# Two running-sum products for each tile's branch, of the tokens' high part and of the rest plus k1 times the first sum, in place of three products of gated operands

## The chip, the cores and the metric

The kernel runs on one core of a Trainium2 chip. A core has TensorE (matrix products into PSUM), VectorE, ScalarE and GpSimd (element-wise work), SyncE (here it only issues DMAs), and DMA engines between the chip's memory (HBM) and the on-chip memory (SBUF). Each engine runs its own list of instructions in order and waits on semaphores for the others. The metric is the device time of one execution in microseconds (us), lower is better.

## The reference

Input are 2048 tokens of 448 channels. With six modulation rows from a conditioning vector `c`, the reference is

```
h = layernorm(x) * (1 + ca) + sa
x = x + ga * (causal_conv(h, K) + h * Dskip)
h = layernorm(x) * (1 + cb) + sb
x = x + gb * ((silu(h @ w_gate) * (h @ w_up)) @ w_down)
```

`K[d, l]` is the real part of a sum over 256 states of `C * dt * B * exp(dt * A * l)`. For inputs whose `dt * A` is very small (the kernel computes a flag for it), `K` is a straight line in `l`: `k0 + k1 * l` for each channel. Then, with t the token of the output and s the token of the input,

```
conv(h)[t] = sum over s <= t of (k0 + k1 * (t - s)) * h[s]
```

which needs only running sums over the tokens. This is the path that runs here. A second path (an FFT by matrix products) lies behind the flag and isn't executed.

## The kernel before

**Tiling.** The 2048 tokens are 16 tiles of 128 tokens, tokens on the partitions and the 448 channels along the row. Tiles go in six blocks (`TILES`): 0-1, 2-3, 4-6, 7-9, 10-12, 13-15. A prologue computes `k0` and `k1` multiplied by the gate `ga` (rows `gm0`, `gm1`, spread over all partitions), the gated skip `gd`, and tiles 0 and 1 entirely up to the transposed operand of the feed-forward part.

**The feed-forward loop.** `run_blocks` calls `ffn` for each block. It has 14 steps f, one for each 128 hidden columns. `gate_up(f)` is 22 matmuls (f32r operands, split into a high and a low part for accuracy) as wide as the block has tokens, 256 or 384; then ScalarE's silu (L773), VectorE's product (L788), ScalarE's cast to the high part `phi` (L795) and VectorE's subtraction for the low part `plo` (L796). `down(f - 1)` is then issued: three 448-wide matmuls for each tile of the block (L808). In the first block the weights arrive during the steps, so that each step also splits weights: ScalarE L115, L122, L123 and VectorE L117 (`wdl`) and L125 (`gu`).

**The branch of the next block** is threaded through these steps. `TIMES` has, for each tile of the next block, a list of half steps h for its stages: an even h places a stage behind `gate_up(h / 2)` and ahead of the `down` that follows it, an odd h behind that `down`. Within one half step the order is tile by tile, then stage by stage. Every engine gets its instructions in exactly this order. The first row of `TIMES` is used while block 0 runs (tiles 2 and 3), the second while block 1 runs (tiles 4 to 6), the third for the later blocks. The last entry of each tile is not a stage but the statistics of its second layernorm.

**The stages before.** `s0` makes the normalized token tile h (VectorE L200, L202, two scalar_tensor_tensor). `s1` makes `v0 = h * gm0` and `v1 = h * gm1` (L957), where row s of `gm0` holds k0 - s * k1 (made once by `gate_0`, L732). `rows` adds to row 0 of both the carried rows (L962, L963). `s2` splits v0 into `vh` (ScalarE L970) and `vl` (VectorE L971). `s3` is h * gd (L976). `s4` multiplies by the triangle of ones `tri`, which is a running sum over the tile's tokens: `vh` and `vl` into the PSUM tile `CV` (L982, L984), `v1` into one of the four rotating PSUM banks (L983); and adds h * gd to x (L985). `s5` copies the last rows, adds them up (L1003, L1004) and sends them by a DMA to partition 0 as the carry for the next tile (L1005; SyncE's queue for tiles 2 and 3, ScalarE's for the others), then adds `o` and `s * token` to x (L1006, L1007).

Which engine multiplies differs by block. While blocks 0 and 1 run, `s1` and `s3` are on VectorE (`v(s1)`, `v(s3)`); later they are on GpSimd. While block 0 runs, tiles 2 and 3 use `s4f`: v0 isn't split but multiplied as full f32 (L995), and v1 as f32r (L994).

**Other names.** `CV` is a single PSUM bank that the branch, `gate_row` and one of the four transposes share. `split_w(j)` and `split_d(j)` split weights, and `pools.load` issues their DMAs on SyncE's queue. `left_over` (name `l1` in `PLAN`) sums `v1` of tiles 0 and 1 for the first carry; `first_rows` and `gate_0` prepare the carry and the gate rows in block 0; `PLAN` is the order of the prologue, written out by hand.

Of the kernel before, what the change touches and what calls it, by code (L numbers as in the profile page):

```python
# [8 lines left out]
F32 = mybir.dt.float32  # L9
F32R = mybir.dt.float32r  # L10
# [33 lines left out]
m1 cpc k1 gd h11 hd0 ck v01 sq0 o10 v10 w0 cbw o12 v11 o01 o02 hd1 w01 o13 o14 fs xh1 gc0 sa d00 gc1 st0 r0 sp x1 st1 r1 l1 spc n10 gq fl n11 D0 qtb sbt sbc  # L44
# [7 lines left out]
def f32(ap):  # L52
    return ap.bitcast(F32)
# [3 lines left out]
def tile_kernel(ctx, tc, x, a_re, a_im, b_re, b_im, c_re, c_im, log_dt,  # L57
# [71 lines left out]
    tok = const.tile([128, 1], F32)  # L129
# [12 lines left out]
    ntok = const.tile([128, 1], F32)  # L142
# [144 lines left out]
    with tc.tile_pool(name="pre", bufs=1) as pre:  # L287
# [20 lines left out]
        po.iota(tok, pattern=[[1, 1]], base=0, channel_multiplier=1, allow_small_or_imprecise_dtypes=True)  # L308
        po.iota(ntok, pattern=[[1, 1]], base=0, channel_multiplier=-1, allow_small_or_imprecise_dtypes=True)
# [25 lines left out]
        for z in range(2):  # L335
# [20 lines left out]
        h01, v0, v1, hd, h2 = ([pre.tile([128, w], t, name=f"{n}_{q}") for q in range(2)] for n, t, w in  # L356
                               (("h", F32, D), ("v0", F32, D), ("v1", F32R, D), ("hd", F32, D), ("h2", F32, 512)))
# [114 lines left out]
        def flag_of():  # L472
# [43 lines left out]
            "fr1": copy(run1[end], CV[end, 0:D]), "fx": copy(xs[0], DN[0][:, 0:D]),  # L516
# [204 lines left out]
    def first_rows():  # L721

        ve.tensor_tensor(run0[end], run1[end], DN[1][end, 0:D], op=OP.add)
# [6 lines left out]
    def gate_0():  # L730

        ve.scalar_tensor_tensor(gm0, gm1, ntok, gm0, op0=OP.mult, op1=OP.add)  # L732

    def run_blocks(pools, stages, first=None):
# [150 lines left out]
        for b, ts in enumerate(TILES):  # L885
            todo = {}
            if b + 1 < len(TILES):
# [53 lines left out]
    def small_path(pools):  # L941
# [10 lines left out]
        def s1(i, on_v=False):  # L952
            h = vs[i]
            v0 = v0_of(i)
            v1 = work.tile([128, D], F32R, name="v1", bufs=2)
            for v, g in ((v0, gm0), (v1, gm1)):
                (ve if on_v else po).tensor_tensor(v, h, g, op=OP.mult)  # L957
            vs[i] = h, v0, v1

        def rows(i):  # L960
            h, v0, v1 = vs[i]
            ve.tensor_tensor(v0[0:1], v0[0:1], run0[0:1], op=OP.add)  # L962
            ve.tensor_tensor(v1[0:1], f32(v1[0:1]), run1[0:1], op=OP.add)  # L963

        def s2(i):
            rows(i)
            h, v0, v1 = vs[i]
            vh = work.tile([128, D], F32R, name="vh")
            vl = work.tile([128, D], F32R, name="vl")
            sc.copy(vh, v0)  # L970
            ve.tensor_tensor(vl, v0, f32(vh), op=OP.subtract)  # L971
            vs[i] = h, vh, vl, v1

        def s3(i, on_v=False):
            h = vs[i][0]
            (ve if on_v else po).tensor_tensor(h, h, gd, op=OP.mult)  # L976

        def s4(i):
            h, vh, vl, v1 = vs[i]
            o = CV[:, 0:D]  # L980
            s = bank()[:, 0:D]
            pe.matmul(o, tri, vh, start=True, stop=False)  # L982
            pe.matmul(s, tri, v1, start=True, stop=True)  # L983
            pe.matmul(o, tri, vl, start=False, stop=True)  # L984
            ve.tensor_tensor(xs[i], h, xs[i], op=OP.add)  # L985
            vs[i] = o, s

        def s4f(i):  # L990
            h, v0, v1 = vs[i]
            o = CV[:, 0:D]
            s = bank()[:, 0:D]
            pe.matmul(s, tri, v1, start=True, stop=True)  # L994
            pe.matmul(o, f32(tri), v0, start=True, stop=True)  # L995
            s3(i, True)
            ve.tensor_tensor(xs[i], h, xs[i], op=OP.add)
            vs[i] = o, s

        def s5(i):  # L1000
            o, s = vs.pop(i)
            if i + 1 < NT:
                sc.copy(run1[end], s[end])  # L1003
                ve.scalar_tensor_tensor(run0[end], run1[end], 128.0, o[end], op0=OP.mult, op1=OP.add)  # L1004
                (sy if i in TILES[1] else sc).dma_start(run[0:1], run[127:128])  # L1005
            ve.tensor_tensor(xs[i], xs[i], o, op=OP.add)  # L1006
            ve.scalar_tensor_tensor(xs[i], s, tok, xs[i], op0=OP.mult, op1=OP.add)  # L1007

        v = lambda g: lambda i: g(i, True)
        return lambda b: ((s0, v(s1), rows, s4f, s5), (s0, v(s1), s2, v(s3), s4, s5),  # L1010
                          (s0, s1, s2, s3, s4, s5))[min(b, 2)]

# [104 lines left out]
```

## Time and profile before

| what | value |
|---|---|
| median of 3 runs (lowest to highest) | 471.73 us (470.73 to 472.09) |
| profiled execution, its own time | 471.05 us |
| its span, first to last instruction | 468.9 us |
| granted TensorE clock, mean | 0.999 |
| end of the prologue, first matmul of the feed-forward part | 31.18 us |
| blocks 0 and 1 (256 tokens each) end at about | 85.5 and 141 us |
| blocks 2, 3, 4 (384 tokens each) end at about | 220.5, 301 and 381.5 us |

The profile's columns: start and duration in us, the engine, the line of the kernel, the operation, output and inputs by the names of the tiles, how many instructions the row merges, and in brackets how long the engine sat idle before it and who released it. Starts of two instructions that follow each other on one engine are often closer than the duration of the first, since instructions overlap in the engine's pipeline; where a stretch of work is added up, the distance of starts is the price.

### The profile page before, as it was taken

How to read it: one execution, taken by the hardware profiler on the slowest of the kernel's cores; microseconds unless marked ns; L12 is line 12 of the kernel's file. 1: busy time of each engine (PE TensorE's matmuls, PEld its weight loads, DVE VectorE, ACT ScalarE, POOL GpSimd, SP SyncE). 2: the span in 40 equal slices, each digit the busy share in tenths (PEclk: the TensorE clock that was granted, in tenths of full speed). 3: DMA queues.
4: the chain of work that ended last, by engine and by line, in shares of the span. 5: the costliest groups of instructions: out<-in, count | busy, mean ns of one | idle time of the engine just before them, and what ended most of it. 6: DMA issues, size and time to landing. Idle time of an engine off the chain costs nothing.

```text
span 468.9 us, 7027 instructions
## 1 busy us (share of the span) xinstructions
PE 459.8 (98%) x2735; PEld 438.2 (93%) x2735; DVE 282.0 (60%) x539; ACT 160.7 (34%) x363; POOL 64.2 (14%) x88
## 2 busy tenths in 40 slices
PE   7899999999999999999999999999999999999995
PEld 5579999999999999999999999999999999999995
DVE  5888999778865547573745756464666553222125
ACT  5888665522243122233212233321223222221111
POOL 2232001000000224100032410004141000000000
PEclk9999999999999999999999999999999999999999
DMA  8966652200003000111300011130000112000001
GB/s 319 404 242 210 219 166 74 67 33 2 2 0 100 0 1 0 46 46 46 117 2 0 2 45 46 45 119 1 1 23 24 46 45 80 22 1 1 1 0 64
DMA packets 18779, 31.24 MB, mean 67 GB/s; under 512 B 2609, under 2 KB 13489, under 8 KB 18737
## 3 DMA queue, kind: packets, MB, share of 16 engines
q1 hardware_dynamic: 18096, 30.53, 18.8%
q8 instruction: 23, 0.38, 0.3%
q10 hardware_dynamic: 640, 0.18, 0.2%
q14 instruction: 20, 0.16, 0.1%
HBM read 24.61 MB, written 6.03 MB: 65 GB/s over the span
## 4 chain that ended last, share of the span: by engine, by line
PE 94%; issue 1%; DVE 1%; DMA 1%; POOL 1%; ACT 1%; DVEq 0%; POOLq 0%; ACTq 0%
PE bank L758 61%; PE dn L808 28%; DMA vec<-in_c_log_dt_dram 1%; PE dn L480 1%; PE bank L983 1%; PE cv L984 1%; PE cv L982 1%; PE bank L227 0%; PE bank L266 0%; DVE x L847 0%; PE bank L403 0%; POOL rsa L186 0%; PE cv L995 0%; PE bank L437 0%; ACT L339 0%
## 5 line engine op out<-in xcount | busy, mean ns | idle before, releaser
L758 PE MATMUL bank<-hhi,gu 128*128 128x384 f32 (+1 forms) x1176 | 208.8, 317 | 0.1
L758 PEld LDWEIGHTS bank<-hhi,gu 128*128 128x128 f32 x1176 | 189.3, 188 | 2.9 <-issue 0.8
L758 PE MATMUL bank<-hlo,gu 128*128 128x384 f32 (+1 forms) x672 | 130.7, 317 | 0.0
L758 PEld LDWEIGHTS bank<-hlo,gu 128*128 128x128 f32 x672 | 109.0, 188 | 0.2
L788 DVE TENSOR_TENSOR bank<-raw,bank 128x384 f32<-128x384 f32 (+1 forms) x69 | 36.9, 534 | 117.5 <-PE bank L758 115.2
L795 ACT CAST phi<-bank 128x384 fp32r<-128x384 f32 (+1 forms) x83 | 36.8, 444 | 138.2 <-DVE bank L788 138.1
L773 ACT ACTIVATE raw<-bank 128x384 f32<-128x384 f32 (+1 forms) x70 | 32.9, 470 | 119.1 <-PE bank L758 103.5
L796 DVE TENSOR_TENSOR plo<-bank,phi 128x384 fp32r<-128x384 f32 (+1 forms) x83 | 42.5, 512 | 37.6 <-ACT phi L795 37.6
L808 PE MATMUL dn<-wdh,phi 128*128 128x448 f32 x218 | 57.6, 365 | 0.0
L808 PE MATMUL dn<-wdh,plo 128*128 128x448 f32 x218 | 57.2, 363 | 0.0
L808 PE MATMUL dn<-wdl,phi 128*128 128x448 f32 x218 | 56.9, 362 | 0.0
L808 PEld LDWEIGHTS dn<-wdh,plo 128*128 128x128 f32 x218 | 40.8, 188 | 3.0 <-DVE plo L796 0.4
L808 PEld LDWEIGHTS dn<-wdl,phi 128*128 128x128 f32 x218 | 40.9, 187 | 2.7
L808 PEld LDWEIGHTS dn<-wdh,phi 128*128 128x128 f32 x218 | 38.7, 188 | 1.6 <-ACT p L773 0.2
L185 POOL TENSOR_SCALAR rsb<-mvb 128x1 f32<-128x1 f32 (+2 forms) x13 | 4.4, 337 | 142.2 <-DVE mvb L157 142.2
L125 DVE TENSOR_TENSOR gu<-raw,gu 128x1024 fp32r<-128x1024 f32 x14 | 17.1, 1220 | 0.9 <-ACT gu L123 0.9
L185 POOL TENSOR_SCALAR rsa<-mva 128x3 f32<-128x3 f32 (+1 forms) x6 | 2.3, 380 | 99.2 <-DVE mva L157 96.9
L957 POOL TENSOR_TENSOR m<-m,gm 128x448 f32<-128x448 f32 x9 | 10.4, 1154 | 20.8 <-DVE m L202 17.1
L971 DVE TENSOR_TENSOR vl<-m,vh 128x448 fp32r<-128x448 f32 x12 | 9.1, 757 | 6.7 <-ACT vh L970 6.1
L122 ACT CAST gu<-raw 128x768 fp32r<-128x768 f32 x14 | 11.7, 832 | 0.0
L976 POOL TENSOR_TENSOR m<-m,gd 128x448 f32<-128x448 f32 x9 | 11.6, 1283 | 0.0
L215 ACT ACTIVATE raw<-raw,rsb 128x64 f32<-128x64 f32 x14 | 4.8, 345 | 18.9 <-DVE raw L212 9.7
(237 smaller groups left out, 413.9 us busy)
## 6 DMA issues: line engine op xcount, KB each, us to landing
raw<-in_B_w_gate_up_dram SPq DMA_DIRECT2D x14, 512.0 KB, 3.6
rawd<-in_B_w_down_dram SPq DMA_DIRECT2D x16, 224.0 KB, 3.8
x<-in_A_u_dram SPq DMA_DIRECT2D x12, 224.0 KB, 2.9
out_dram<-x SPq DMA_DIRECT2D x11, 224.0 KB, 2.0
xd<-raw SPq DMA_DIRECT2D x9, 256.0 KB, 2.1
raw<-xd SPq DMA_DIRECT2D x36, 64.0 KB, 1.9
wm<-in_w_mod_groups_dram SPq DMA_DIRECT2D x5, 448.0 KB, 8.2
wm<-in_w_mod_groups_dram SPq DMA_DIRECT2D x5, 336.0 KB, 8.2
```

The lines of the kernel that those rows point to most:

```text
L122: sc.copy(wgu[j][:, :, 0:3, :], w[:, :, 0:3, :])
L125: ve.tensor_tensor(wgu[j][:, :, 3:7, :], w[:, :, ::-1, :], f32(wgu[j][:, :, 0:4, :][:, :, ::-1, :]), op=OP.subtract)
L185: po.tensor_scalar(rs[:, 0:n], self.mv[:, 0:n, 1], EPS, None, op0=OP.add)
L758: pe.matmul(ps[s][:, 0:n], w[:, s, a], (hlo if lo else hhi)[:, k, first_col(n):first_col(n) + n], start=first and q == 0, stop=end and q = ...
L773: sc.activation(p[:, 0:n], ps[0][:, 0:n], AF.Silu)
L788: ve.tensor_tensor(ps[1][:, 0:n], p[:, 0:n], ps[1][:, 0:n], op=OP.mult)
L795: sc.copy(hi[:, 0:n], ps[1][:, 0:n])
L796: ve.tensor_tensor(lo[:, 0:n], ps[1][:, 0:n], f32(hi[:, 0:n]), op=OP.subtract)
L808: pe.matmul(dn[q][:, 0:D], u[:, cs], v, start=f == 0 and z == 0, stop=f == (NF - 3 if last else NF - 1) and z == 2)
L957: (ve if on_v else po).tensor_tensor(v, h, g, op=OP.mult)
L971: ve.tensor_tensor(vl, v0, f32(vh), op=OP.subtract)
L976: (ve if on_v else po).tensor_tensor(h, h, gd, op=OP.mult)
```

## The change

For each tile the two sums are now chained. With u the running sum of h, the convolution is (k0 - k1) * u[t] + k1 * (running sum of u)[t]. So:

- `s1` (GpSimd, all blocks): `v0 = h * gd`.
- `s2`: the carried row is added to row 0 of h (VectorE), `hh` is the high part of h (ScalarE cast), and h becomes the rest, h - hh (VectorE).
- `s3` (GpSimd): the rest is multiplied by `gm0`, and `v0` is added to x.
- `s4`: one product, `u = tri * hh`, into `CV`.
- `s5`: VectorE makes `t = u * gm1`, `w = t + h` (the gated rest) and adds the second carried row to row 0 of w; the first carry (last row of u) is copied and sent; VectorE makes `t = u * gma` with gma = gm0 - gm1, and GpSimd adds it to x.
- `s6`: the second product, `v = tri * w`, into the same `CV`.
- `s7`: the second carry (last row of v) is copied and sent, and VectorE adds v to x.

All blocks use this list; the variants by block are gone, and so are the index columns `tok` and `ntok`. Two carries are sent for each tile, of one row each, in place of one of two rows. In the prologue, two casts `hh0` and `hh1` on ScalarE feed `left_over`; `gate_0` is three GpSimd instructions in place of one on VectorE; the DMA of the first carry is issued at step 2 in place of step 0. `TIMES` has eight stages for each tile:

```
-    ((1, 3), 5, ((5, 10, 13, 15, 15, 16), (9, 9, 17, 19, 20, 20)), 20, (22, 23)),
-    ((2, 3, 3), 3, ((5, 6, 8, 10, 10, 11, 13), (7, 8, 14, 15, 17, 17, 18), (13, 17, 17, 18, 20, 21, 21)), 23, (23, 23, 23)),
-    ((2, 3, 3), 3, ((5, 6, 8, 9, 10, 11, 12), (7, 8, 13, 14, 15, 16, 17), (11, 12, 18, 18, 20, 21, 21))),
+    ((1, 3), 5, ((5, 6, 10, 11, 12, 12, 14, 15, 16), (9, 10, 14, 15, 16, 16, 18, 20, 20)), 20, (22, 23)),
+    ((2, 3, 3), 3, ((5, 5, 8, 8, 10, 10, 12, 13, 13), (7, 8, 12, 12, 14, 14, 16, 17, 18), (11, 12, 16, 16, 18, 18, 20, 21, 21)),
+     23, (23, 23, 23)),
+    ((2, 3, 3), 3, ((5, 5, 8, 8, 10, 10, 12, 13, 13), (7, 8, 12, 12, 14, 14, 16, 17, 17), (11, 12, 16, 16, 18, 18, 20, 21, 21))),
...
+    gma = const.tile([128, D], F32)
...
-                pe.matmul(CV[:, 0:D], all1, v1[q], start=q == 0, stop=q == 1)
+                pe.matmul(CV[:, 0:D], all1, hh[q], start=q == 0, stop=q == 1)
...
-            "fr1": copy(run1[end], CV[end, 0:D]), "fx": copy(xs[0], DN[0][:, 0:D]),
+            **{f"hh{q}": copy(hh[q], h01[q]) for q in range(2)}, "fr1": copy(run0[end], CV[end, 0:D]), "fx": copy(xs[0], DN[0][:, 0:D]),
...
-        ve.tensor_tensor(run0[end], run1[end], DN[1][end, 0:D], op=OP.add)
+        ve.tensor_copy(run1[end], DN[1][end, 0:D])
...
-        ve.scalar_tensor_tensor(gm0, gm1, ntok, gm0, op0=OP.mult, op1=OP.add)
+        t = v0_of(2)[end]
+        po.tensor_tensor(gma, gm0, gm1, op=OP.subtract)
+        po.tensor_tensor(t, run0[end], gma[end], op=OP.mult)
+        po.tensor_tensor(run1[end], run1[end], t, op=OP.subtract)
...
-                    at(0, 1, lambda: sy.dma_start(run[0:1], run[127:128]))
+                    at(2, 1, lambda: sy.dma_start(run[0:1], run[127:128]))
...
+        def s1(i):
+            po.tensor_tensor(v0_of(i), vs[i], gd, op=OP.mult)
+
+        def s2(i):
             h = vs[i]
+            ve.tensor_tensor(h[0:1], h[0:1], run0[0:1], op=OP.add)
+            hh = work.tile([128, D], F32R, name="hh")
+            sc.copy(hh, h)
+            ve.tensor_tensor(h, h, f32(hh), op=OP.subtract)
+            vs[i] = h, hh
+
+        def s3(i):
             h = vs[i][0]
+            po.tensor_tensor(h, h, gm0, op=OP.mult)
+            po.tensor_tensor(xs[i], xs[i], v0_of(i), op=OP.add)
 
         def s4(i):
+            h, hh = vs[i]
+            u = CV[:, 0:D]
+            pe.matmul(u, tri, hh, start=True, stop=True)
+            vs[i] = h, u
+
+        def carry(i, k, row):
+            if i + 1 < NT:
+                sc.copy(run[end, k, :], row[end])
+                (sy if i in TILES[1] else sc).dma_start(run[0:1, k, :], run[127:128, k, :])
 
         def s5(i):
+            h, u = vs[i]
+            t = work.tile([128, D], F32, name="t")
+            w = work.tile([128, D], F32R, name="w")
+            ve.tensor_tensor(t, u, gm1, op=OP.mult)
+            ve.tensor_tensor(w, t, h, op=OP.add)
+            ve.tensor_tensor(w[0:1], f32(w[0:1]), run1[0:1], op=OP.add)
+            carry(i, 0, u)
+            ve.tensor_tensor(t, u, gma, op=OP.mult)
+            po.tensor_tensor(xs[i], xs[i], t, op=OP.add)
+            vs[i] = w
+
+        def s6(i):
+            v = CV[:, 0:D]
+            pe.matmul(v, tri, vs[i], start=True, stop=True)
+            vs[i] = v
+
+        def s7(i):
+            v = vs.pop(i)
+            carry(i, 1, v)
+            ve.tensor_tensor(xs[i], xs[i], v, op=OP.add)
+
+        return lambda b: (s0, s1, s2, s3, s4, s5, s6, s7)
```

More of the change, by code (lines that the diff above doesn't have):

```diff
@@ L128, in tile_kernel @@
     tri = const.tile([128, 128], F32R)
-    tok = const.tile([128, 1], F32)
     run = const.tile([128, 2, D], F32)
@@ L141, in tile_kernel @@
     mhalf, half = halves[:, 0:1], halves[:, 1:2]
-    ntok = const.tile([128, 1], F32)
     pick = const.tile([128, 1], F32)
@@ L355, in tile_kernel @@
         sca = pre.tile([128, N], F32)
-        h01, v0, v1, hd, h2 = ([pre.tile([128, w], t, name=f"{n}_{q}") for q in range(2)] for n, t, w in
-                               (("h", F32, D), ("v0", F32, D), ("v1", F32R, D), ("hd", F32, D), ("h2", F32, 512)))
+        h01, v0, v1, hd, hh, h2 = ([pre.tile([128, w], t, name=f"{n}_{q}") for q in range(2)] for n, t, w in
+                               (("h", F32, D), ("v0", F32, D), ("v1", F32R, D), ("hd", F32, D), ("hh", F32R, D), ("h2", F32, 512)))
         qt = {n: pre.tile([128, 512], F32, name="qt" + n) for n in "gcs"}
@@ L948, in s0 @@
             vs[i] = h
-        def s1(i, on_v=False):
+        def s1(i):
+            po.tensor_tensor(v0_of(i), vs[i], gd, op=OP.mult)
+        def s2(i):
             h = vs[i]
[L954 to L974, printed above, removed]
+            ve.tensor_tensor(h[0:1], h[0:1], run0[0:1], op=OP.add)
+            hh = work.tile([128, D], F32R, name="hh")
+            sc.copy(hh, h)
+            ve.tensor_tensor(h, h, f32(hh), op=OP.subtract)
@@ L975, in s3 @@
+            vs[i] = h, hh
+        def s3(i):
             h = vs[i][0]
-            (ve if on_v else po).tensor_tensor(h, h, gd, op=OP.mult)
+            po.tensor_tensor(h, h, gm0, op=OP.mult)
+            po.tensor_tensor(xs[i], xs[i], v0_of(i), op=OP.add)
         def s4(i):
[L979 to L998, printed above, removed]
-        def s5(i):
[L1001 to L1007, printed above, removed]
```

7 lines of the change are left out of this document (1 added, 6 removed).

## The prediction

> **What bounds the kernel now.** I read the page's totals first, then its slices.
>
> ```profile
> PE 459.8 (98%) x2735; PEld 438.2 (93%) x2735; DVE 282.0 (60%) x539; ACT 160.7 (34%) x363; POOL 64.2 (14%) x88
> ...
> PE   7899999999999999999999999999999999999995
> ...
> DVE  5888999778865547573745756464666553222125
> ...
> PE bank L758 61%; PE dn L808 28%; DMA vec<-in_c_log_dt_dram 1%; PE dn L480 1%; PE bank L983 1%; PE cv L984 1%; PE cv L982 1%; PE bank L227 0%; PE bank L266 0%; DVE x L847 0%; PE bank L403 0%; POOL rsa L186 0%; PE cv L995 0%; PE bank L437 0%; ACT L339 0%
> ```
>
> TensorE is the bound from 31 us to the end: the chain is its own matmuls, and the branch's products (L982 to L984, L995) lie on it. Whatever leaves TensorE's list shortens the kernel by its full length, and whatever makes TensorE wait lengthens it. VectorE's 60% is a mean: in slices 3 to 7 (35 to 82 us) it is at 7 to 9 tenths. So I asked for the windows of the blocks.
>
> ```profile
> 31.00:85.50 54.50, 54.37 (x398) 51.66 (x398) 50.68 (x92) 39.11 (x91) 5.42 (x10) 1.00 0.47 154
> 85.50:141.00 55.50, 55.49 (x414) 54.06 (x414) 42.78 (x88) 18.25 (x46) 2.23 (x4) 1.00 0.07 22
> 141.00:220.50 79.50, 79.50 (x440) 77.82 (x439) 44.57 (x81) 20.97 (x44) 14.72 (x17) 1.00 0.11 35
> ```
>
> After the length come TensorE, weight loads, VectorE, ScalarE and GpSimd in us. In block 0 VectorE works 50.7 of 54.5 us, in block 1 42.8 of 55.5, in block 2 44.6 of 79.5. TensorE waits in none of them, and GpSimd does 5.4 and 2.2 us in the first two.
>
> **What it removes: 3.5 us of TensorE.** The chain in order of time gives the steps, and TensorE's timeline the products.
>
> ```profile
> 50.01 2.51 PE bank L758 x22
> 52.52 1.20 PE dn L808 x6
> ...
> 59.93 1.20 PE dn L808 x6
> 61.34 0.75 PE cv L995 x2
> 62.09 2.60 PE bank L758 x22
> ...
> 174.15 1.80 PE dn L808 x9
> 175.95 3.81 PE bank L758 x22
> ```
> ```profile
> 127.58 0.37 PE L982 MATMUL cv<-vh,tri 128*128 128x448 f32 x1
> 127.78 0.36 PE L983 MATMUL bank<-v,tri 128*128 128x448 f32 x1
> ...
> 128.18 0.56 PE L808 MATMUL dn<-wdh,phi 128*128 128x448 f32 x2
> ...
> L984 PE MATMUL cv<-vl,tri 128*128 128x448 f32 x12 | 4.4, 364 | 0.0
> ```
>
> Starts are 0.20 us apart (three products in 0.60), so a product of this kind costs 0.20, three of them 0.60; the new pair has the same shape and type and costs 0.40. Tiles 4 to 15 (x12) save 12 x 0.20 = 2.4 us. Tiles 2 and 3 spend from 59.93 + 1.20 = 61.13 to 62.09, 0.96, and would spend 0.40: 2 x 0.56 = 1.1. Together 3.5 us.
>
> **What it adds on VectorE: a chain between two products.** Before, the products of a tile follow each other. Now the second needs `t`, `w` and the row of `w`, which VectorE can only begin behind the `plo` of that step. The prices, start to start:
>
> ```profile
> 50.83 0.68 DVE L200 SCALAR_TENSOR_TENSOR m<-x,mva,ca 128x448 f32<-128x448 f32 x1
> ...
> 52.26 0.63 DVE L957 TENSOR_TENSOR m<-m,gm 128x448 f32<-128x448 f32 x1
> ...
> 53.34 0.62 DVE L117 TENSOR_TENSOR wdl<-rawd,wdh 128x448 fp32r<-128x448 f32 x1
> ...
> 54.20 1.22 DVE L125 TENSOR_TENSOR gu<-raw,gu 128x1024 fp32r<-128x1024 f32 x1
> ...
> 55.67 0.62 DVE L957 TENSOR_TENSOR m<-m,gm 128x448 f32<-128x448 f32 x1
> ...
> 70.63 1.23 DVE L125 TENSOR_TENSOR gu<-raw,gu 128x1024 fp32r<-128x1024 f32 x1 [0.45 <-ACT gu L123]
> ...
> 105.55 0.60 DVE L962 TENSOR_TENSOR m<-m,run 1x448 f32<-1x448 f32 x1
> ...
> 107.33 0.62 DVE L957 TENSOR_TENSOR m<-m,gm 128x448 f32<-128x448 f32 x1
> ...
> 108.40 0.42 DVE L788 TENSOR_TENSOR bank<-raw,bank 128x256 f32<-128x256 f32 x1
> ...
> 109.60 0.62 DVE L976 TENSOR_TENSOR m<-m,gd 128x448 f32<-128x448 f32 x1
> 110.25 0.63 DVE L985 TENSOR_TENSOR rawd<-m,rawd 128x448 f32<-128x448 f32 x1
> ```
>
> `make_h` costs 1.43 (50.83 to 52.26). Block 0's own work of a step costs 2.33 (53.34 to 55.67), block 1's 1.20 (108.40 to 109.60, with the wait for the cast). Row, cast on ScalarE and rest cost about 1.78 (105.55 to 107.33, two rows then, of which the second ran under the cast). A 448-wide instruction costs 0.54, or 0.66 behind one that it depends on (109.60 to 110.25).
>
> *Block 0*, from `make_h` of tile 3 at 50.83 to the end of tile 3's row of `w`: 1.43; step 5's own work 2.33; tile 2's row, cast and rest 1.78; step 6 2.33; `t`, `w`, row, `t` again 0.66 + 0.66 + 0.53 + 0.54 = 2.39; step 7 2.33; tile 3's row, cast and rest 1.78; x + v 0.54; step 8 2.33; `t`, `w` and the row's end 1.92. That is 19.2 us, or 70.0; plus 0.45 twice, since the cast `hh` waits in ScalarE's list ahead of the weight splits that VectorE needs (the 0.45 at 70.63 is such a wait): 70.9. TensorE would want that product (`s6`, behind `gate_up(9)`) at 52.52 + 4 x 3.71 + 3 x 0.20 = 68.0. **2.9 us late**, shared out over the products on the way.
>
> *Block 1*, counted from the end of `gate_up(5)`, a step being 3.71 + 0.20: 0.1, own work 1.20, tile 4's 2.39, `make_h` of tile 6 1.43, step 6's 1.20, tile 5's row to rest 1.78, then x + v of tile 4, which ends at 8.7. Tile 5's first product writes `CV`, which that addition still reads, and is wanted at 7.8: 0.9 late. The same sum goes on without another wait until tile 6's first product, 0.2 late. **1.1 us.**
>
> *Later blocks*: a step is 5.62 + 0.20. Own work with 384 columns is about 1.20 x 384 / 256 = 1.8 us, the chain 1.92: 2 us of room, which hold tile by tile what else a half step carries. Nothing.
>
> **What it moves to GpSimd.** Four GpSimd instructions of 448 elements for each tile, where blocks 0 and 1 had none. What happens when both engines read SBUF:
>
> ```profile
> 185.07 1.16 POOL L957 TENSOR_TENSOR v<-m,g 128x448 fp32r<-128x448 f32 x1
> 185.54 1.16 DVE L971 TENSOR_TENSOR vl<-m,vh 128x448 fp32r<-128x448 f32 x1 [1.48 <-ACT vh L970]
> 186.18 1.55 POOL L976 TENSOR_TENSOR m<-m,gd 128x448 f32<-128x448 f32 x1
> ...
> L971 DVE TENSOR_TENSOR vl<-m,vh x12: 624/626/1162, 106.8 to 362.2; 128x448 fp32r<-128x448 f32 x12
> ...
> 21.95 1.14 POOL L478 TENSOR_TENSOR hd<-h,gd 128x448 f32<-128x448 f32 x1 [3.36 <-ACT gd L481]
> ...
> 22.60 1.15 DVE L478 TENSOR_TENSOR v<-h,dn 128x448 fp32r<-128x448 f32 x2
> ```
>
> The rest took 1.162 in place of 0.626 beside a GpSimd instruction, and the next GpSimd instruction 1.55 in place of 1.16: VectorE loses 0.54 at a meeting. An operand in PSUM avoids it (22.60: two in 1.15, GpSimd's unhurt). Between 52 and 70 us six of the GpSimd instructions run (`s1` of tile 3, `s3` twice for both tiles, x + t of tile 2), and VectorE is never idle for long: 6 x 0.54 = **3.2 us**. In block 1 VectorE's SBUF-only instructions (row, rest, `w`, row, about 2.1 us of a step of 3.9) fill half the time, and there is room in some steps, so I take half of the delay as reaching a product: 12 x 0.5 x 0.54 x 0.5 = **1.6 us**. Bounds: 0, and every meeting at its full 1.15, 6.9 and 3.5 us. I take 0.54, since L971 is the very instruction.
>
> **Small parts.**
>
> ```profile
> 25.20 0.60 ACT L115 CAST wdh<-rawd 128x448 fp32r<-128x448 f32 x1
> 25.66 0.56 ACT L481 COPY g<-dn 128x448 f32<-128x448 f32 x1
> 27.30 0.54 ACT L395 COPY qts<-bank 128x448 f32<-128x448 f32 x1 [1.07 <-PE bank L269]
> ...
> DMA to landing us min/median/max: 1.6/1.7/3.3
> ...
> 176.53 0.50 ACTq L1005 DMA_DIRECT2D run<-run  x1
> ```
>
> The two prologue casts (0.46 each) fit into ScalarE's 1.07 of idle time behind 25.66: 0 to 0.1. `gate_0` goes from VectorE to GpSimd ahead of the stretch summed above; uncovered it would be three meetings, 3 x 0.54 = 1.6. The carries of tiles 2 and 3 go through SyncE's queue, behind the weight loads, which wait for VectorE's splits. The first one, moved behind the loads of step 2, has 9 us until tile 2's row at 54.6 (50.83 + 1.43 + 2.33). Tile 2's first carry follows two loads that wait for step 6's split, which ends at about 58.7: issued at about 60, landed by 61.7, or 63.3 at the slowest landing, and VectorE comes to tile 3's row at 63.4. Nothing, with 0.1 left at the slowest. Later carries are issued by ScalarE, 0.50 us each, one more for each tile, beside its copy of a row; behind them in its list stands the next silu, and ScalarE is busy 18.25 of block 1's 55.5 us, so it has the time. Nothing.
>
> **Sum.** -3.5 + 2.9 + 3.2 + 1.1 + 1.6 = +5.3 on the profiled execution's 471.05, that is 476.4. The median of the runs is 0.68 above that execution: **477.0**.
>
> **Rivals.** *All waits are hidden:* VectorE keeps ahead of `s6` of tile 3, and the 3.5 us are gained whole: 471.73 - 3.5 = 468.2. For it: VectorE has fewer instructions for tiles 2 and 3 (seven in place of nine, `make_h` aside), and TensorE waits nowhere today. It decides at one point, whether the 20.1 us from 50.8 to 70.9 become less than 17.2. Against it: they are measured distances, and VectorE's list has no gap.
>
> *GpSimd costs VectorE nothing*, its instructions falling beside operands in PSUM or waits: -3.5 + 2.9 + 1.1 = +0.5, 472.2. Against it are the 1162 ns.
>
> *GpSimd costs its full length*, always starting first: 2.9 + 6.9 + 1.1 + 3.5 - 3.5 = +10.9, 482.6. For it: the 185.54 row ends 0.47 after GpSimd's 186.23, so VectorE seems to stand still until GpSimd is done. The Trainium skill (SBUF — State Buffer, section "Who interferes with whom") has this as a lock: a VectorE instruction with two SBUF inputs and a GpSimd instruction that reads SBUF exclude each other, and the later one waits for the whole of the earlier. By that rule the loss is anything up to 1.15 each, and it speaks against moving these products to GpSimd beside a full VectorE; the trace agrees for L971.
>
> **Chances.** 477.0: 55%. All hidden: 15%. GpSimd free: 17%. Full length: 13%. 0.3% is 1.4 us, about what can be told from no change: 470.3 to 473.1. The second rival lies in it about half of the time, else mostly above. Slower 74%, same 9%, faster 17%. Range 468.0 to 483.0, from the first rival to the last, about 13% left out.
>
> **What would show it.** Right: the products of `tri` 0.20 apart and two for each tile; TensorE idle in blocks 0 and 1 ahead of `s4` and `s6`, released by VectorE, some 6 and 3 us in all, and none later; VectorE without gaps from 50 to 75 us; VectorE's `wdl`, `gu` and rest stretched beside GpSimd. Wrong: no idle TensorE in block 0 (the first rival), idle time without stretched instructions (the second), waits released by a carry's DMA, or idle time in the later blocks.

## The result, and the profile after

| | before | after |
|---|---|---|
| median of the runs | 471.68 us (4 runs, 470.73 to 472.09) | 479.26 us (4 runs, 478.9 to 480.76) |
| ratio, 95% interval | | 1.0168 [1.0155, 1.0181] |
| profiled execution, its own time and span | 471.05, 468.9 | 479.35, 477.6 |

The change costs 7.6 us; 477.0 was predicted (468 to 483). The page of the changed kernel first: its totals, the slices of TensorE and VectorE, and the chain that ended last.

```profile
PE 457.5 (96%) x2721; PEld 435.4 (91%) x2721; DVE 281.6 (59%) x526; ACT 171.1 (36%) x380; POOL 102.7 (21%) x118
...
PE   6899978999899999999999999999999999999995
...
DVE  4888988766866446774653776365477544222225
...
PE 83%; DVE 10%; issue 4%; ACT 2%; DMA 1%; POOL 0%; DVEq 0%; ACTq 0%; POOLq 0%
```

TensorE has 2.3 us less to do than before (457.5 against 459.8), and yet the span grew. The chain says how: a tenth of it is now VectorE, which held 1% of the chain before. TensorE's row has new dents in its 6th, 7th and 11th slices (60 to 84 and 119 to 131 us), which lie in blocks 0 and 1. The windows at the same borders as before show the same; after the length come TensorE, weight loads, VectorE, ScalarE and GpSimd in us.

```profile
31.00:85.50 54.50, 48.55 (x350) 45.58 (x349) 48.64 (x79) 38.80 (x89) 21.15 (x21) 1.00 0.48 154
85.50:141.00 55.50, 52.24 (x386) 50.36 (x385) 39.47 (x78) 18.33 (x44) 15.05 (x14) 1.00 0.07 22
141.00:220.50 79.50, 79.50 (x465) 77.81 (x464) 46.30 (x87) 25.45 (x53) 18.97 (x22) 1.00 0.09 28
```

TensorE now stands idle for 5.95 us in the first window and 3.26 in the second, and for nothing in the third. VectorE is no busier in them (48.6 and 39.5 us, where it was 50.7 and 42.8): it isn't fuller, it is late, and part of its work now falls behind the window's end. GpSimd went from 5.4 to 21.2 us and from 2.2 to 15.1.

For the bill by blocks I took three marks: the first matmul of the feed-forward part, and the start of the long `down` (x12) that ends each block, from the chain in order of time. Those of before:

```profile
85.49 2.42 PE dn L808 x12
...
141.02 2.40 PE dn L808 x12
```

and those of after:

```profile
92.26 2.41 PE dn L809 x12
...
151.34 2.41 PE dn L809 x12
```

With the first matmul from TensorE's timeline and the last addition from VectorE's, after:

```profile
32.06 1.89 PE L759 MATMUL bank<-hhi,gu 128*128 128x256 f32 x14
```
```profile
472.63 0.36 DVE L848 TENSOR_TENSOR x<-dn,x 128x192 f32<-128x192 f32 x1
```

and the last addition of before:

```profile
464.14 0.36 DVE L847 TENSOR_TENSOR x<-dn,x 128x192 f32<-128x192 f32 x1
```

| stretch | before | after | difference |
|---|---|---|---|
| block 0 | 85.49 - 31.18 = 54.31 | 92.26 - 32.06 = 60.20 | +5.89 |
| block 1 | 55.53 | 59.08 | +3.55 |
| blocks 2 to 4 and the tail | 323.12 | 321.29 | -1.83 |

-1.83 is the nine tiles prepared from block 2 on, 9 x 0.20 us: there the change does just what it was costed at. (The prologue is 0.88 longer in this one profile. Among the kernels below, with nearly the same prologue, the first matmul starts anywhere between 31.07 and 32.77, so that isn't counted.) Of the saving of 3.5 us, 1.1 lies in block 0 and 0.6 in block 1, so what was lost is 5.89 + 1.1 = 7.0 and 3.55 + 0.6 = 4.15 us: **11.15 us against the 8.8 predicted.**

Every wait of TensorE in these blocks, from its timeline, with the idle time and its releaser in brackets:

```profile
40.12 0.97 PE L759 MATMUL bank<-hhi,gu 128*128 128x256 f32 x6 [0.23 <-DVE gu L126]
...
58.61 0.48 PE L972 MATMUL cv<-hh,tri 128*128 128x448 f32 x1 [0.85 <-ACT hh L960]
...
64.68 0.47 PE L994 MATMUL cv<-w,tri 128*128 128x448 f32 x1 [1.80 <-DVE t L988]
...
70.10 0.48 PE L972 MATMUL cv<-hh,tri 128*128 128x448 f32 x1 [1.23 <-DVE x L1000]
...
76.07 0.47 PE L994 MATMUL cv<-w,tri 128*128 128x448 f32 x1 [1.70 <-DVE t L988]
...
119.35 0.47 PE L994 MATMUL cv<-w,tri 128*128 128x448 f32 x1 [0.74 <-DVE t L988]
...
125.03 0.47 PE L972 MATMUL cv<-hh,tri 128*128 128x448 f32 x1 [1.49 <-DVE rawd L1000]
...
129.54 0.48 PE L994 MATMUL cv<-w,tri 128*128 128x448 f32 x1 [0.32 <-DVE t L988]
...
138.44 0.47 PE L994 MATMUL cv<-w,tri 128*128 128x448 f32 x1 [0.70 <-DVE t L988]
```

L972 is the first product of a tile (`s4`), L994 the second (`s6`). All rows but the first are the branch's products. The releaser of the second is the surprise: not the row of `w` (L986), its operand, but L988, which is `t = u * gma`. That instruction reads `CV`, and the second product writes `CV`. The prediction had priced L988 as work, but let the product start at the row's end.

The brackets add up to 9.1 us, less than the 11.15 that were lost, since a wait costs more than its bracket. The matmuls ahead of the product at 58.61 start at 57.14, and an unhindered group of the same kind is followed after 0.46 (55.89 to 56.35): the product is 1.01 late where the bracket says 0.85. The next matmul then follows after 0.32 in place of 0.20. That is 0.28 more for this wait, and nine such waits make 2.5 us, enough for the gap.

VectorE's timeline around the first four of the branch's waits, and GpSimd's beside it:

```profile
48.63 1.85 DVE L126 TENSOR_TENSOR gu<-raw,gu 128x1024 fp32r<-128x1024 f32 x1
...
55.24 1.85 DVE L126 TENSOR_TENSOR gu<-raw,gu 128x1024 fp32r<-128x1024 f32 x1
...
60.47 1.38 DVE L126 TENSOR_TENSOR gu<-raw,gu 128x1024 fp32r<-128x1024 f32 x1 [0.38 <-ACT gu L124]
...
62.11 0.61 DVE L984 TENSOR_TENSOR t<-cv,g 128x448 f32<-128x448 f32 x1
...
64.02 0.60 DVE L988 TENSOR_TENSOR t<-cv,gma 128x448 f32<-128x448 f32 x1
...
65.43 1.83 DVE L126 TENSOR_TENSOR gu<-raw,gu 128x1024 fp32r<-128x1024 f32 x1
...
69.97 1.17 DVE L118 TENSOR_TENSOR wdl<-rawd,wdh 128x448 fp32r<-128x448 f32 x1
...
71.48 1.75 DVE L126 TENSOR_TENSOR gu<-raw,gu 128x1024 fp32r<-128x1024 f32 x1
```
```profile
47.92 1.47 POOL L954 TENSOR_TENSOR m<-m,gd 128x448 f32<-128x448 f32 x1 [0.89 <-DVE m L202]
54.61 1.41 POOL L954 TENSOR_TENSOR m<-m,gd 128x448 f32<-128x448 f32 x1 [5.21 <-DVE m L202]
59.30 1.47 POOL L966 TENSOR_TENSOR m<-m,gm 128x448 f32<-128x448 f32 x1 [3.28 <-DVE m L961]
60.73 2.14 POOL L967 TENSOR_TENSOR x<-x,m 128x448 f32<-128x448 f32 x1
64.77 1.40 POOL L989 TENSOR_TENSOR x<-x,t 128x448 f32<-128x448 f32 x1 [1.90 <-DVE t L988]
69.51 1.14 POOL L966 TENSOR_TENSOR m<-m,gm 128x448 f32<-128x448 f32 x1 [3.34 <-DVE m L961]
70.61 1.54 POOL L967 TENSOR_TENSOR x<-x,m 128x448 f32<-128x448 f32 x1
```

A weight split (L126) that took 1.22 us before takes 1.85 (twice), 1.38, 1.83 and 1.75, a `wdl` 1.17 in place of 0.62. From 55 us on these are five rows, in which VectorE loses 0.63 + 0.16 + 0.61 + 0.55 + 0.53 = 2.5 us; the split at 48.63 loses 0.63 more, 3.1 in all. `t` at 62.11, which reads PSUM, runs beside GpSimd's addition at its usual 0.61.

The rows also show what one meeting costs. The split at 55.24 finds a GpSimd instruction that runs until 56.02, 0.78 longer, and loses 0.63; the one at 60.47 finds 0.30 left (59.30 + 1.47) and loses 0.16. In all six rows the loss is what was left of GpSimd's instruction, less 0.13 to 0.15. So the price hangs on how long before VectorE's instruction GpSimd's began.

In block 1 only two of the branch's rows are stretched, `w` and the second instruction of tile 6's `make_h` (0.69 at 105.67 in the same profile):

```profile
116.74 1.38 DVE L985 TENSOR_TENSOR w<-t,m 128x448 fp32r<-128x448 f32 x1
...
119.92 1.46 DVE L202 SCALAR_TENSOR_TENSOR m<-m,rsa,sa 128x448 f32<-128x448 f32 x1
```
```profile
116.48 1.15 POOL L954 TENSOR_TENSOR m<-m,gd 128x448 f32<-128x448 f32 x1
119.44 1.46 POOL L989 TENSOR_TENSOR rawd<-rawd,t 128x448 f32<-128x448 f32 x1 [1.80 <-DVE t L988]
```

They lose 0.75 and 0.77, 1.5 us together.

### The profile page after: what moved, and what is told of

Read it like the earlier page. It is cut to its first block, busy times and chain, and to the rows that moved or that the text cites. A ratio compares the mean times of both kernels' runs of the same rounds, so it can differ in the third digit from the quotient of the medians.

```text
span 477.6 us, 7099 instructions
## 1 busy us (share of the span) xinstructions
PE 457.5 (96%) x2721; PEld 435.4 (91%) x2721; DVE 281.6 (59%) x526; ACT 171.1 (36%) x380; POOL 102.7 (21%) x118
## 4 chain that ended last, share of the span: by engine, by line
PE 83%; DVE 10%; issue 4%; ACT 2%; DMA 1%; POOL 0%; DVEq 0%; ACTq 0%; POOLq 0%
PE bank L759 53%; PE dn L809 25%; DVE gu L126 2%; DVE w L985 1%; DVE bank L789 1%; DMA vec<-in_c_log_dt_dram 1%; DVE plo L797 1%; PE cv L994 1%; PE dn L478 1%; DVE t L984 1%; DVE t L988 1%; DVE wdl L118 1%; ACT phi L796 0%; DVE w L986 0%; DVE x L825 0%
## 5 line engine op out<-in xcount | busy, mean ns | idle before, releaser
L966 POOL TENSOR_TENSOR m<-m,gm 128x448 f32<-128x448 f32 x14 | 16.5, 1177 | 71.2 <-DVE m L961 71.2
L126 DVE TENSOR_TENSOR gu<-raw,gu 128x1024 fp32r<-128x1024 f32 x14 | 20.4, 1458 | 1.4 <-ACT gu L124 1.4
L954 POOL TENSOR_TENSOR m<-m,gd 128x448 f32<-128x448 f32 x14 | 16.7, 1194 | 18.3 <-DVE m L202 18.3
L989 POOL TENSOR_TENSOR x<-x,t 128x448 f32<-128x448 f32 x10 | 12.8, 1279 | 30.6 <-DVE t L988 30.6
L977 ACT COPY run<-cv 32x448 f32<-32x448 f32 x26 | 13.7, 526 | 11.5 <-DVE t L984 9.3
L960 ACT CAST hh<-m 128x448 fp32r<-128x448 f32 x14 | 7.9, 566 | 17.9 <-DVE m L958 17.9
L961 DVE TENSOR_TENSOR m<-m,hh 128x448 f32<-128x448 f32 x14 | 8.8, 625 | 8.9 <-ACT hh L960 8.9
```

Source lines behind the costliest of these rows:

```text
L126: ve.tensor_tensor(wgu[j][:, :, 3:7, :], w[:, :, ::-1, :], f32(wgu[j][:, :, 0:4, :][:, :, ::-1, :]), op=OP.subtract)
L954: po.tensor_tensor(v0_of(i), vs[i], gd, op=OP.mult)
L961: ve.tensor_tensor(h, h, f32(hh), op=OP.subtract)
L966: po.tensor_tensor(h, h, gm0, op=OP.mult)
L977: sc.copy(run[end, k, :], row[end])
L989: po.tensor_tensor(xs[i], xs[i], t, op=OP.add)
```

## The experiments

Two theories were put against each other. One: the loss is VectorE's order, and what GpSimd does beside it, in two shares of about the same size. The other: GpSimd alone (its meetings, or its results coming late), or the order alone. Each block length below is taken at the marks of the table above, from one profile of each kernel. Such lengths are good to a few tenths only: a step of block 0 in which TensorE waits for nothing lasts 3.70 us in most places and up to 3.81 in others, and the places differ from profile to profile.

**Without GpSimd's instructions for tiles 2 to 6.**

```
         def s1(i):
-            po.tensor_tensor(v0_of(i), vs[i], gd, op=OP.mult)
+            if i > 6:
+                po.tensor_tensor(v0_of(i), vs[i], gd, op=OP.mult)
...
```

> The changed kernel without the four GpSimd instructions of tiles 2 to 6 (h * gd, rest * gm0, x + v0, x + t are left out there). VectorE, TensorE and the half steps stay. TensorE waits 5.7 us in block 0 and 3.2 us in block 1 of the changed kernel's trace. Theory (VectorE is late by the order of its list, and more so by its meetings with GpSimd; 0.54 for each of some 9 meetings): the stretched weight splits go back to 1.22, the waits become about 4 us, the time falls by about 5, to 474.5. Rival (order and the reuse of the PSUM tile CV alone): GpSimd's absence changes nothing, 479. Rival (each meeting at its full 1.15): the waits become under 2 us, 472.

475.36 us (4 runs), ratio to before 1.0092 [1.0062, 1.0121]. Block 0 lasts 57.75 us (2.45 less than in the changed kernel), block 1 57.09 (1.99 less). So GpSimd's work costs 4.4 us by the blocks and 3.9 by the medians, where 4.8 were predicted. Of the 3.1 us that the six rows of block 0 lost, 2.45 came back. Block 1's 1.99 is more than the 1.5 that its two rows lost; one of TensorE's waits there is gone with them. The larger part, 6.7 us, stays without it. One stretched weight split is left, beside `gate_0`, which this kernel keeps; the view of that line gives the shortest, median and longest duration in ns:

```profile
L126 DVE TENSOR_TENSOR gu<-raw,gu x14: 1214/1222/1995, 24.7 to 81.6; 128x1024 fp32r<-128x1024 f32 x14
```

**GpSimd's results unused.** The work stays; tiles 2 to 6 write the last three results into `v0`, which neither VectorE nor TensorE reads.

```
-            po.tensor_tensor(h, h, gm0, op=OP.mult)
-            po.tensor_tensor(xs[i], xs[i], v0_of(i), op=OP.add)
+            po.tensor_tensor(v0_of(i) if i < 7 else h, h, gm0, op=OP.mult)
+            po.tensor_tensor(v0_of(i) if i < 7 else xs[i], xs[i], v0_of(i), op=OP.add)
...
```

> The changed kernel with the GpSimd instructions of tiles 2 to 6 in place, reading the same operands, but writing the last three into v0, where nothing needs them (the rest isn't gated and the skip and x + t are left out there). So nothing waits for GpSimd, while its reads stand beside VectorE's as before. Theory (the 3.9 us that the kernel without these instructions gained are meetings of the two engines): the time stays, 479. Rival (VectorE's w and x + v waited for GpSimd's results): as without the instructions, 475.4.

480.0 us (4 runs), 1.019 [1.017, 1.0209]; blocks 60.07 and 59.30. Nothing came back. The rest `w` is stretched up to 1633 ns:

```profile
L985 DVE TENSOR_TENSOR w<-t,m x14: 625/626/1633, 61.9 to 369.1; 128x448 fp32r<-128x448 f32 x14
```

So the 4.4 us are the meetings of the two engines, and no wait for what GpSimd computes. The order in which both engines use `x` is kept here, but it isn't the cause either: in blocks 0 and 1 VectorE's list has one wait that GpSimd ends, at `x + v` of tile 6 behind the last of the branch's products, 0.19 us in the changed kernel and 0.20 in this one.

**The kernel before, with its products on GpSimd in blocks 0 and 1.**

```
-        v = lambda g: lambda i: g(i, True)
-        return lambda b: ((s0, v(s1), rows, s4f, s5), (s0, v(s1), s2, v(s3), s4, s5),
+        return lambda b: ((s0, s1, rows, s4f, s5), (s0, s1, s2, s3, s4, s5),
...
```

> The kernel before, with its products h * gm0, h * gm1 and h * gd on GpSimd in blocks 0 and 1 too, where it had them on VectorE; nothing else changes. Theory (GpSimd beside a full VectorE costs what it saves, and each product comes 1.15 in place of 0.62 later): TensorE, which waits nowhere in these blocks before, waits some 2 us, 473.7. Rival (GpSimd is free): VectorE is relieved by 15 x 0.54 = 8 us in these blocks and no product is late, 471.7. Rival (full length): over 476.

472.01 us (10 runs), 1.0007 [0.9997, 1.0016]: no cost, and a miss for the theory. TensorE waits nowhere in these blocks, though the profiled execution was the longest of the ten, 474.04. The meetings are there, on both sides:

```profile
L125 DVE TENSOR_TENSOR gu<-raw,gu x14: 1206/1218/1790, 25.0 to 80.2; 128x1024 fp32r<-128x1024 f32 x14
```
```profile
L976 POOL TENSOR_TENSOR m<-m,gd x14: 1151/1466/3960, 60.3 to 359.3; 128x448 f32<-128x448 f32 x14
```

but VectorE has handed over three instructions of 0.6 us for each tile, and I take this to be the room that the meetings use. Of these two kernels, the meetings cost time in the one in which TensorE already waits for VectorE.

**The second product in a bank of its own.**

```
         def s6(i):
-            v = CV[:, 0:D]
+            v = bank()[:, 0:D]
```

> The changed kernel with the second product v in a rotating PSUM bank of its own in place of CV. In the changed kernel's trace the second products wait for the second t (which reads u in CV), and the first product of the next tile waits for x + v (which reads v in CV). Theory (VectorE's list is late as a whole, so TensorE waits for the next thing on it): only the distance from the row of w to the second t, 0.54, is saved where nothing else is late, about 1 to 1.5 us, 478. Rival (the reuse of CV is the main cause): the waits for x + v, 1.23 and 1.49, and 5 x 0.54 are gone, 5.4 us, 474. Rival (no part in it): 479.3.

478.39 us (4 runs), 1.0137 [1.0118, 1.0156]; blocks 59.77 and 58.12, 0.43 and 0.96 less, and 0.9 less by the medians. Of TensorE's waits, by line and releaser (us in total, times, longest):

```profile
PE bank L994 <- DVE w L986: 4.1, 3, 2.5
...
PE bank L994 <- ACT raw L774: 1.5, 2, 1.2
```

L988 is gone from the list, and the row of `w` has taken its place, as it should; but twice the product now waits for ScalarE's silu to leave the rotating bank. The waits of a first product for x + v (L1000) are gone too, since that addition no longer reads `CV`. So 0.9 to 1.4 us come back for both readers of `CV` together, not five times the 0.54 that L988 takes.

**The parts of what is left without GpSimd.** The next three start from the first experiment: with the second product's own bank, without `gate_0`, and both.

```
         def s6(i):
-            v = CV[:, 0:D]
+            v = bank()[:, 0:D]
```

> This kernel leaves out the four GpSimd instructions of tiles 2 to 6 (as the run without them did, 475.36 us) and also gives the second product a bank of its own, so that it doesn't wait until t = u * gma has read CV. What is left is VectorE's order alone. If the CV read makes up the missing part of the order's term (about 1.4 us by the run with an own bank and GpSimd's work in place), this comes to 474.0 to 474.4; if the rotating banks are busy at that point and the product waits for them, it stays at 475.0 or more. Block 0 56.9 to 57.4 us (57.75 without the bank), block 1 56.0 to 56.5 (57.09).

```
         def gate_0():
-            t = v0_of(2)[end]
-            po.tensor_tensor(gma, gm0, gm1, op=OP.subtract)
-            po.tensor_tensor(t, run0[end], gma[end], op=OP.mult)
-            po.tensor_tensor(run1[end], run1[end], t, op=OP.subtract)
+            pass
...
+        po.memset(gma, 0.0)
```

> This kernel leaves out the four GpSimd instructions of tiles 2 to 6 and also the three of gate_0 (gma is set to zero in the prologue, and run1 keeps its first value). If gate_0's meetings with the first weight splits cost 0.5 us at the start of block 0 (VectorE's split there took 1.99 us in place of 1.22, and TensorE waits 0.23 us for it), this comes to 474.8 to 475.0 and the longest split falls from 1.99 to 1.23 us; if gate_0 costs nothing, 475.36. The prediction had put nothing for it.

> This kernel leaves out the four GpSimd instructions of tiles 2 to 6 and the three of gate_0 (gma is set to zero in the prologue, run1 keeps its first value), and gives the second product its own bank: what is left of the change's cost is VectorE's order as the prediction counted it. If that order's sums (2.9 us in block 0, 1.1 in block 1) were right for what they counted, and the read of CV and gate_0 add up without overlap, block 0 lasts 54.31 - 1.1 + 2.9 = 56.1 us, block 1 55.53 - 0.6 + 1.1 = 56.0, and the time is 472.4 to 473.2, 3.5 less than the 2.9 + 1.1 above it, so 0.5 above before, plus what the single pieces differ. If the two pieces overlap, block 0 is 56.5 to 56.8 us and the time 473.5 or more.

| kernel | median (runs) | ratio to before | block 0 | block 1 |
|---|---|---|---|---|
| without GpSimd's work | 475.36 (4) | 1.0092 [1.0062, 1.0121] | 57.75 | 57.09 |
| and the second product's own bank | 473.55 (7) | 1.0075 [1.0042, 1.0108] | 57.14 | 56.34 |
| and `gate_0` left out instead | 474.15 (6) | 1.0057 [1.0041, 1.0072] | 56.79 | 57.21 |
| both | 473.59 (12) | 1.0043 [1.0029, 1.0057] | 56.38 | 56.30 |

The medians hardly tell the last three apart (the runs of the second kernel reach from 473.31 to 478.74, which is why its ratio is the higher one), so the parts rest on the block lengths. By these the own bank is worth 0.61 and 0.75 us, `gate_0` 0.96 in block 0 and nothing in block 1. Together they take 1.37 off block 0, a little less than the sum of 1.57. Of the 0.96, about 0.2 is not `gate_0`: steps without any wait are longer in the first profile by that much (two of them 3.81 and 3.79 us, where the other has 3.71). The expectation had left two outcomes for the last kernel, 56.1 and 56.5 to 56.8 us in block 0; 56.38 lies between. Its runs scatter from 472.15 to 475.12, and the profiled one is the lowest; so its median agrees with the second outcome and its profile with neither. I use the block lengths, with that reserve.

`gate_0` was put at nothing in the prediction. GpSimd's timeline of the changed kernel, and the two VectorE instructions beside it:

```profile
34.55 2.01 POOL L732 TENSOR_TENSOR m<-run,gma 32x448 f32<-32x448 f32 x1 [2.77 <-ACT run L479]
...
37.85 1.14 POOL L733 TENSOR_TENSOR run<-run,m 32x448 f32<-32x448 f32 x1 [1.29 <-ACT wdh L116]
```
```profile
35.79 1.25 DVE L118 TENSOR_TENSOR wdl<-rawd,wdh 128x448 fp32r<-128x448 f32 x1
...
38.08 1.99 DVE L126 TENSOR_TENSOR gu<-raw,gu 128x1024 fp32r<-128x1024 f32 x1
```

Two meetings, of 0.63 and 0.77 us, at the first splits of the block. TensorE waits for that at once (its 40.12 row): from the first `down` to the second it takes 4.65 us in the kernel without GpSimd's work (37.68 to 42.33), and 4.06 without `gate_0` as well (38.22 to 42.28). Without `gate_0` the longest split is 1.23 us:

```profile
L126 DVE TENSOR_TENSOR gu<-raw,gu x14: 1216/1220/1227, 25.3 to 81.2; 128x1024 fp32r<-128x1024 f32 x14
```

**Other half steps.** If a product waits only since too few half steps lie between it and the one before, spreading the stages ends the waits. Block 1's row of `TIMES` alone:

```
-    ((2, 3, 3), 3, ((5, 5, 8, 8, 10, 10, 12, 13, 13), (7, 8, 12, 12, 14, 14, 16, 17, 18), (11, 12, 16, 16, 18, 18, 20, 21, 21)),
+    ((2, 3, 3), 3, ((3, 3, 5, 8, 8, 9, 11, 11, 13), (5, 7, 11, 11, 13, 13, 16, 17, 19), (11, 12, 15, 15, 18, 18, 21, 21, 21)),
```

> The changed kernel with other half steps for tiles 4 to 6 (second row of TIMES): (3, 3, 5, 8, 8, 9, 11, 11, 13), (5, 7, 11, 11, 13, 13, 16, 17, 19), (11, 12, 15, 15, 18, 18, 21, 21, 21). The second product stands 3 half steps behind the first in place of 2, so that it follows two gate_up in place of one for two of the tiles. Theory (block 1's waits are a matter of distance, VectorE being busy 43 of 64 us there): all of them go, the block's 59.1 us become 55.5 - 0.6 = 54.9, 4.2 us less, 475.1; block 0 stays. Rival (VectorE has too much to do in block 1 too): the waits move to other places, 478 to 479.

476.99 us (4 runs), 1.0112 [1.009, 1.0134]. Block 1 falls from 59.08 to 56.2 us, with one branch wait of 0.31 left of four: 2.9 us by the block, 2.3 by the medians. And block 0's row alone:

```
-    ((1, 3), 5, ((5, 6, 10, 11, 12, 12, 14, 15, 16), (9, 10, 14, 15, 16, 16, 18, 20, 20)), 20, (22, 23)),
+    ((1, 3), 5, ((5, 8, 10, 12, 12, 12, 14, 15, 17), (7, 11, 12, 17, 17, 18, 21, 21, 21)), 21, (22, 23)),
```

> The changed kernel with other half steps for tiles 2 and 3 alone: (5, 8, 10, 12, 12, 12, 14, 15, 17) and (7, 11, 12, 17, 17, 18, 21, 21, 21), root of the second layernorm at 21. The same instructions. Theory (VectorE has too much to do from step 5 on, so spacing helps only in part): block 0's waits fall from 5.8 to about 3.5 us, 477. Rival (distance alone): they go, 473.6. Rival (amount alone): 479.

478.22 us (4 runs), 1.0144 [1.0127, 1.0161]. Block 0 still lasts 58.95 us. Two of the branch's waits are gone, but others have come, by TensorE's timeline:

```profile
65.26 0.47 PE L994 MATMUL cv<-w,tri 128*128 128x448 f32 x1 [1.88 <-DVE t L988]
...
70.61 0.68 PE L809 MATMUL dn<-wdh,phi 128*128 128x448 f32 x2 [1.15 <-ACT phi L796]
...
71.94 0.67 PE L809 MATMUL dn<-wdh,plo 128*128 128x448 f32 x2 [0.25 <-DVE plo L797]
```

`down` itself now waits. In block 1 the distance was missing; in block 0, at least with these half steps, the delay only changes the product that meets it. I take VectorE to have too much to do at that place; no third spacing was run.

**Less work for VectorE in block 0.** Tiles 2 and 3 keep one full f32 product for `u`, so that hh, the rest and its gate fall away; x + v0 and x + t go back to VectorE, so that of GpSimd's four instructions one is left; the second product stays.

```
+        def s4f(i):
+            u = CV[:, 0:D]
+            pe.matmul(u, f32(tri), vs[i], start=True, stop=True)
...
+        def s5f(i):
...
+            ve.tensor_tensor(w, u, gm1, op=OP.mult)
...
+        return lambda b: (s0, s1, s2, s3, s4, s5, s6, s7) if b else (s0, s1, rowf, s3f, s4f, s5f, s6, s7)
```

Its half steps in block 0 are (6, 6, 10, 11, 13, 13, 16, 16, 19) and (11, 14, 15, 17, 19, 19, 21, 21, 21).

> The changed kernel with another form for tiles 2 and 3 alone: u is one full f32 product of h (as L995 was before, 0.75), so there is no cast hh, no rest and no gating of it, and VectorE makes w from u in one instruction; x + v0 and x + t are on VectorE, only h * gd stays on GpSimd; half steps (6, 6, 10, 11, 13, 13, 16, 16, 19) and (11, 14, 15, 17, 19, 19, 21, 21, 21). Theory (block 0's loss is VectorE's late list, lengthened by the chain hh - rest - gated rest and its meetings): block 0 takes as long as before, 54.3 in place of 60.2 us, 473.4 in all; block 1 keeps its waits. Rival (two products one behind the other can't be hidden in block 0 whatever VectorE does): still some 3 us of waits, 476.

473.54 us (5 runs), 1.0042 [1.0027, 1.0058]. Block 0 lasts 54.50 us, as before, with no wait but the one for the early split:

```profile
39.91 0.97 PE L759 MATMUL bank<-hhi,gu 128*128 128x256 f32 x6 [0.26 <-DVE gu L126]
```

This kernel changes three things at once in block 0 (the chain, GpSimd's share and the half steps); how much each of them gave was not measured.

Block 1 keeps its four waits and 59.12 us. With half steps for block 1 of (5, 6, 6, 7, 8, 8, 12, 12, 14), (6, 6, 12, 12, 14, 15, 17, 17, 18) and (10, 11, 17, 17, 18, 19, 21, 21, 21) added:

> As the kernel with the full f32 product u for tiles 2 and 3, and tiles 4 to 6 at (5, 6, 6, 7, 8, 8, 12, 12, 14), (6, 6, 12, 12, 14, 15, 17, 17, 18), (10, 11, 17, 17, 18, 19, 21, 21, 21). Theory: with the waits gone in both blocks only TensorE's saving is left, 12 tiles x 0.20 = 2.4 us, since tiles 2 and 3 now cost 0.95 as before: 471.7 - 2.4 = 469.3, faster than both. Rival (the waits come back elsewhere): 471 or more.

470.10 us (12 runs, 468.67 to 472.63), 0.9969 [0.9951, 0.9986]: 0.3% faster than the kernel before. The last wait was the early split, so `gate_0` goes from half step 1 to 4:

```
-EXTRA = (1,)
+EXTRA = (4,)
```

> The re-spaced kernel with a full f32 product of h in block 0 (470.10 us), with gate_0 at half step 4 in place of 1, behind the first and fullest steps. If gate_0 costs 0.5 us only since it stands where VectorE is late anyway, this comes to 469.6 and the wait of 0.26 us at about 39 us is gone; if the meetings only move to the next splits, 470.1 as before, with a wait a step later.

**469.05 us (6 runs, 468.69 to 470.19), 0.9953 [0.9938, 0.9969].** TensorE waits for nothing between 30 and 160 us, and its windows are as full as in the kernel before:

```profile
31.00:85.50 54.50, 54.37 (x402) 51.93 (x401) 50.10 (x87) 41.28 (x96) 13.45 (x15) 1.00 0.50 154
85.50:141.00 55.50, 55.35 (x412) 53.78 (x411) 38.86 (x80) 20.10 (x49) 15.91 (x16) 1.00 0.07 22
```

From its first feed-forward matmul at 31.50 to its last addition at 462.12 it takes 430.62 us, where the kernel before takes 432.96: 2.34 less, the 12 x 0.20 of tiles 4 to 15. Against the step before it, 430.95 us in the profile, the late `gate_0` is worth 0.33; the two intervals overlap, so that step rests on the profile and the wait that is gone.

## Why the prediction came out as it did

| term | predicted | measured | by |
|---|---|---|---|
| saving of TensorE | -3.5 | -1.83 for nine tiles; the other 1.7 taken as costed | table by blocks |
| VectorE's order | 2.9 + 1.1 | 3.2 + 1.4 | "both": 56.38 - (54.31 - 1.1), 56.30 - (55.53 - 0.6) |
| meetings with GpSimd in the branch | 3.2 + 1.6 | 2.45 + 1.99 | without GpSimd's work |
| the shared bank `CV`, and `gate_0` | 0, but for x + v in block 1's 1.1 | 1.4 + 0.8 | without GpSimd's work, less "both" |
| sum | +5.3 | +7.7 (medians: +7.6) | -3.5 + 4.6 + 4.4 + 2.2 |

The measured parts come from single profiles. From the medians the three costs are 5.4 (order), 3.9 (meetings) and 1.8 (bank and `gate_0`): the same total of +7.6, and the same ranking, but with the order's term further above its 4.0. The first two together cost 9.0 to 9.3 us, and 8.8 were predicted; how the total splits among the three is good to about 1 us.

**The saving** was right: 9 x 0.20 is what the later blocks gained, and the last kernel's 2.34 is what twelve tiles would give. The 1.1 of tiles 2 and 3 was not measured alone.

**The order** was right as a mechanism and in its place. The dents are in blocks 0 and 1 and nowhere later, and VectorE releases TensorE. Its list isn't quite without gaps, as the prediction had it: it waits 0.63 and 0.69 us for the cast `hh`, which the 1.78 contained. The two sums were 0.6 us short together by the blocks, 1.4 by the medians. That TensorE stands idle 5.95 and 3.26 us, where "some 6 and 3 us" were written down, is partly luck: the prediction meant by it the time lost, and that was 7.0 and 4.15, since a wait costs more than its bracket. In block 1 the sum named the right wait: without GpSimd's work, tile 5's first product waits for x + v for 0.64 in the bracket, about 0.9 lost, and 0.9 was predicted. The second one, tile 6's first product, never waited. With the second product's own bank the wait for x + v is gone and the second products wait for `w` instead (0.94 and 0.20), so the 1.4 of the table are other waits than those counted.

**The meetings** were right as a mechanism; their sum, 4.4 or 3.9 in place of 4.8, is near partly by luck. In block 0 five of the six priced instructions stretch a row, by 0.16 to 0.63 us and not 0.54 each, and `s1` of tile 2, which wasn't counted, stretches a sixth. In block 1 half of twelve meetings were priced at half their delay; there are two, of 0.75 and 0.77, and both reach a product whole. The Trainium skill's rule (SBUF — State Buffer, "Who interferes with whom") is that a VectorE instruction with two SBUF inputs and a GpSimd instruction that reads SBUF exclude each other, and the later one waits. The trace agrees: the loss is the rest of the GpSimd instruction, less 0.13 to 0.15 in block 0. The stretches reach from 0.16 to 1.01 us (`w` at 1633 ns in place of 626), so "all at full length", the third rival, was too dear.

**The step that was mis-sized** is the point at which the product may start. The prediction ended tile 3's chain with "`t`, `w` and the row's end", and named `CV` as a bank only where tile 5's first product overwrites what x + v reads. But `s6` overwrites what `t = u * gma` reads in the same way, one instruction behind the row, and all five waits of a second product in the changed kernel end with that read. A bank of its own takes off 0.4 to 0.6 us in block 0 and 0.75 to 0.9 in block 1, the end of the waits for x + v included. The second half of it is `gate_0`, which the text put "ahead of the stretch summed above", and so at nothing: 0.7 to 1.0 us. It is ahead of that stretch, but not ahead of work that TensorE waits for. Its own bound, three meetings uncovered for 1.6, would have held it; two of the three stretch a VectorE instruction.

**The rest.** The carries cost nothing: in the changed kernel no wait of TensorE behind the prologue is released by a DMA. The rival "all hidden" fell with the dents, "GpSimd free" with the first experiment. In the kernel before, moving the products to GpSimd did cost nothing.

## What to carry to other kernels

Where two products of one chain share a PSUM bank, as here, the second starts behind the last read of the first one's result, not behind its own operand: list each reader before a wait is priced. Moving work from VectorE to GpSimd was paid for here where VectorE was late, in stretched neighbours and not in waits for results; count it at the instructions that TensorE waits for, by what is left of GpSimd's instruction when VectorE's begins. When a re-spaced schedule moves a wait from one product to another without ending it, suspect that there is too much work at that place, and try less of it: in block 0 less work with other half steps ended the waits, where other half steps alone did not.

## What was not expected of the hardware

A GpSimd instruction over 32 partitions was no shorter than one over 128: of `gate_0`'s two 32x448 instructions the one that began before its neighbour on VectorE took 1.14 us, and its 128x448 one 1.13. The other began behind VectorE's and took 2.01: GpSimd, too, loses at a meeting when it comes second. Its 128x448 product took up to 3.96 us in the kernel before with its products moved; VectorE waited 0.73 us for it there, and TensorE not at all. And a row addition on one partition (`w` L986, 1x448) takes VectorE 0.61 us, as long as a whole tile.
